# LayerNorm and MLP on one core: the first token tile in smaller pieces, b1 transposed first, and a first wave of five weight rows

## The chip, the core and the metric

The kernel runs on one core of a Trainium2 chip. A core has five engines that run their own instruction queues side by side: TensorE (PE, matrix multiplies into the accumulation memory PSUM, here eight banks), VectorE (DVE), ScalarE (ACT), GpSimd (POOL) and SyncE (SP, which here issues DMAs). Engines wait for each other and for DMAs by semaphores. The metric is the device time of one execution in microseconds (us); lower is better. The times of the kernel before are 399.81, 400.02 and 400.22 us, median 400.02.

## The reference

```python
y = _layernorm(x, axis=-1)                                    # x: 1 x 2048 x 1024, eps 1e-5
h = _gelu(jnp.einsum("bsd,df->bsf", y, w1) + b1)              # w1: 1024 x 3584, tanh form of gelu
return jnp.einsum("bsf,fd->bsd", h, w2) + b2                  # w2: 3584 x 1024
```

All inputs and the output are bfloat16. Counted in 128 x 128 blocks, the tokens make 16 tiles, the model dimension 8 contraction blocks (dt, 0 to 7) of the first product, and the hidden dimension 28 "rows" (r).

## The kernel before

Tokens are taken in four blocks of 512, each four tiles of 128. For a block, the first product computes for every hidden row r the 128 x 512 result sum over dt of w1[dt, r] against the transposed normalised tokens yT[dt], eight matmuls of 512 columns (line 354). ACT applies bias and GELU from PSUM into hT (L364). Then the second product (L397) runs, for each tile and each half of the 1024 outputs, 28 matmuls over the hidden rows; DVE adds b2 and stores to o_sb (L408), SP writes it out (L413). Five PSUM banks (ps_1, NB1) rotate for the first product, two (ps_2, NB2) for the second, and one (ps_t) takes transposes of the first block.

The program is first written as five lists of operations, one per engine, with named events; waits become semaphore waits when the lists are emitted. So the order in each list is the order in which the engine runs, and an operation that waits holds all behind it.

Block 0, the head, is special. Its four tiles arrive by their own DMAs. `SP_FIRST_LOADS` and `ACT_FIRST_LOADS` are the orders in which the SP and ACT queues issue the first loads; x0a and x0b are the column halves of tile 0, w0 to w3 are quarters of the first 512 columns of w1 (two column halves times two halves of dt). `ln_seq` puts the LayerNorm on DVE: for each tile two statistics (L253, one per column half) and an aggregate (L260); POOL raises to the power -0.5 (L257); then a subtract-and-multiply norm in place (L264). The norm of a tile stands on DVE behind the first statistics of the next tile:

```python
for h in range(2):
    seq.append(op_stats(i, h))
    if h == 0 and prev is not None:
        seq += ops_norm(prev)
seq.append(op_aggr(i))
```

Tile 0 is normalised in two halves of 512 columns, the others in one instruction of 1024. PE transposes a tile's eight 128 x 128 pieces into PSUM (L327, `pe_T`), and ACT copies them in two halves of 512 columns to yT (L333). PE also transposes b1 (L429), which ACT copies (L431), and runs warm-up matmuls on ones (L419): 26 free ones and then 8, 8 and 6 gated on steps of tile 0's LayerNorm.

The first product of block 0 starts with a "wave": four rows (`R_WAVE`), each with its own bank, are computed tile by tile with 128-column matmuls, so that work can start when one tile is there. For each tile, PE does the first four contraction blocks of the four rows, then the transposes of the next tile, then the other four blocks. The first matmul of each row of the wave waits for b1's copy as well. From row 4 on whole rows of 512 columns follow. Later blocks are normalised and transposed on DVE (L305) in gaps; a planner merges these operations with the evictions L408 by estimated due times (`est`, `pe_t`, `T_PE_START`). After the first loads, SP issues the rest of w1, x of block 1, w2, b2 and the other x.

## Time and profile before

| what | value |
|---|---|
| runs | 399.81, 400.02, 400.22 us |
| profiled execution, first to last instruction (span) | 398.3 us |
| median of the runs less that span | 1.7 us |
| PE busy | 394.9 us, 99% |
| PE on L354 and on L397 | 194.8 and 194.2 us |
| DVE, ACT, POOL busy | 137.3, 82.3, 9.7 us |
| DMA | 23.64 MB, most of it in the first 55 us |

The page gives no other time of the profiled execution than its span. The busy time of PE is modelled with pipelined ends, so it is read here by starts: how far two matmuls start apart. The stretch that matters is the first 16 us; all times in the text are counted from the first instruction of the profiled execution. "Landing" of a DMA is the time at which its semaphore is full.

### The profile page before, as it was taken

Reading aid. Unit: us, or ns where it says so; the run is one execution under the profiler, and the core shown is the slowest. Engines: PE = TensorE matmul, PEld = TensorE weight load, DVE = VectorE, ACT = ScalarE, POOL = GpSimd, SP = SyncE. Lnnn points to the kernel's source line nnn. Section 1 sums busy time; section 2 is a strip of 40 time slices with the busy share of each in tenths; the row PEclk is TensorE's granted clock in tenths of the full one; section 3 lists DMA queues with packets and bytes.
Section 4 is the critical chain, followed back from the end, with each engine's and each line's share of the span. In section 5 each row is a group of like instructions: output and inputs, shape, how many; then the busy total and the mean of one; then the engine's idle time right before and its main releaser. Section 6 shows DMA issues by size and latency. Waiting matters only on the chain.

```text
span 398.3 us, 4699 instructions
## 1 busy us (share of the span) xinstructions
PE 394.9 (99%) x2056; PEld 189.4 (48%) x2056; DVE 137.3 (34%) x292; ACT 82.3 (21%) x122; POOL 9.7 (2%) x25
## 2 busy tenths in 40 slices
PE   8999999999999999999999999999999999999998
PEld 7744444444444444444444444444444444444447
DVE  5207999899892004988100000001100000001011
ACT  3544430000044332000024334100003344400000
POOL 2002000200010000000000000000000000000000
DMA  8999930000000000000000000000000000000001
GB/s 255 369 387 386 385 146 15 26 13 29 26 1 2 0 0 2 26 15 26 27 15 0 0 2 0 1 27 26 13 28 13 2 0 0 2 13 26 15 26 28
DMA packets 17614, 23.64 MB, mean 59 GB/s; under 512 B 1466, under 2 KB 10042, under 8 KB 17594
## 3 DMA queue, kind: packets, MB, share of 16 engines
q1 hardware_dynamic: 17162, 22.95, 16.6%
q10 hardware_dynamic: 432, 0.39, 0.3%
q8 instruction: 16, 0.26, 0.3%
q14 instruction: 4, 0.03, 0.0%
HBM read 19.14 MB, written 4.19 MB: 59 GB/s over the span
## 4 chain that ended last, share of the span: by engine, by line
PE 99%; ACT 0%; issue 0%; DVE 0%; POOL 0%; POOLq 0%
PE ps L354 49%; PE ps L397 49%; PE ps L419 1%; PE ps_t L327 0%; ACT yT_sb L333 0%; DVE o_sb L408 0%; POOL ones L244 0%; ACT b_sb L431 0%; POOLq L525 0%
## 5 line engine op out<-in xcount | busy, mean ns | idle before, releaser
L354 PE MATMUL ps<-yT_sb,w_sb 128*128 128x512 bf16 (+1 forms) x992 | 194.8, 358 | 0.5 <-ACT b_sb L431 0.5
L397 PE MATMUL ps<-w_sb,hT_sb 128*128 128x512 bf16 (+1 forms) x980 | 194.2, 361 | 0.0
L354 PEld LDWEIGHTS ps<-yT_sb,w_sb 128*128 128x128 bf16 x992 | 91.7, 98 | 102.4 <-ACT b_sb L431 0.7
L397 PEld LDWEIGHTS ps<-w_sb,hT_sb 128*128 128x128 bf16 x980 | 91.3, 98 | 102.6
L364 ACT ACTIVATE hT_sb<-ps,b_sb 128x512 bf16<-128x512 f32 x112 | 76.7, 688 | 257.2 <-PE ps L354 257.2
L305 DVE STREAM_TRANSPOSE yT_sb<-x_sb 32x256 bf16<-32x256 bf16 x192 | 83.7, 436 | 35.0 <-PE ps L354 32.1
L408 DVE TENSOR_TENSOR o_sb<-ps,b_sb 128x512 bf16<-128x512 f32 (+1 forms) x35 | 22.6, 645 | 197.9 <-PE ps L397 197.8
L253 DVE BATCH_NORM_STATS2 st_sb<-x_sb 128x6 f32<-128x512 bf16 x32 | 21.1, 671 | 21.4 <-DMA x_sb<-in_x_dram 21.2
L257 POOL TENSOR_TENSOR rstd_sb<-mv_sb,nhalf 128x1 f32<-128x1 f32 x16 | 8.8, 551 | 111.5 <-DVE mv_sb L260 111.5
L264 DVE TENSOR_SCALAR x_sb<-x_sb,mv_sb,rstd_sb 128x1024 bf16<-128x1024 bf16 (+1 forms) x17 | 8.9, 528 | 3.7 <-POOL rstd_sb L257 2.7
L419 PE MATMUL ps<-ones 128*128 128x128 bf16 x51 | 5.4, 290 | 1.0 <-POOL ones L244 1.0
L419 PEld LDWEIGHTS ps<-ones 128*128 128x128 bf16 x51 | 4.6, 135 | 1.5 <-POOL ones L244 1.0
L333 ACT COPY yT_sb<-ps_t 128x512 bf16<-128x512 bf16 x7 | 3.8, 589 | 7.0 <-PE ps_t L327 7.0
L260 DVE BATCH_NORM_AGGREGATE mv_sb<-st_sb 128x2 f32<-128x15 f32 x16 | 3.6, 222 | 1.5
L327 PE MATMUL ps_t<-ident,x_sb 128*128 128x128 bf16 x28 | 2.2, 220 | 0.0
L422 ACT ACT_TABLE_LOAD x1 | 1.3, 1283 | 2.2 <-issue 2.2
L327 PEld LDWEIGHTS ps_t<-ident,x_sb 128*128 128x128 bf16 x28 | 1.7, 98 | 0.1
L333 ACT COPY yT_sb<-ps 128x512 bf16<-128x512 bf16 x1 | 0.6, 591 | 0.0
L327 PE MATMUL ps<-ident,x_sb 128*128 128x128 bf16 x4 | 0.4, 222 | 0.0
L245 POOL TENSOR_SCALAR_AFFINE_SELECT ident<-ones 128x128 bf16<-128x128 bf16 x1 | 0.3, 294 | 0.1
L327 PEld LDWEIGHTS ps<-ident,x_sb 128*128 128x128 bf16 x4 | 0.2, 98 | 0.1
L244 POOL MEMSET ones<- 128x128 bf16 x1 | 0.2, 205 | 0.3 <-POOLq L525 0.3
(10 smaller groups left out, 1.2 us busy)
## 6 DMA issues: line engine op xcount, KB each, us to landing
w_sb<-in_w_dram SPq DMA_DIRECT2D x4, 1792.0 KB, 18.5
w_sb<-in_w_dram SPq DMA_DIRECT2D x2, 2048.0 KB, 16.7
out_dram<-o_sb SPq DMA_DIRECT2D x31, 128.0 KB, 1.7
x_sb<-in_x_dram SPq DMA_DIRECT2D x3, 1024.0 KB, 14.2
w_sb<-in_w_dram SPq DMA_DIRECT2D x2, 1024.0 KB, 9.2
w_sb<-in_w_dram SPq DMA_DIRECT2D x4, 256.0 KB, 4.7
x_sb<-in_x_dram SPq DMA_DIRECT2D x2, 256.0 KB, 4.4
x_sb<-in_x_dram ACTq DMA_DIRECT2D x3, 128.0 KB, 3.7
```

The source lines that it names most:

```text
L253: return (lambda e, i=i, h=h: e.bn_stats(st_sb[:, i, 6 * h:6 * (h + 1)], x_sb[:, i, h * HC:(h + 1) * HC]), [x_ev[i][h]], f"st{i}_{h}", 0.65)
L257: pool.op(lambda e, i=i: e.tensor_tensor(out=rstd_sb[:, i:i + 1], in0=mv_sb[:, i, 1:2], in1=nhalf[:, i:i + 1], op=ALU.pow), waits=[f"mv{i} ...
L260: return (lambda e, i=i: e.bn_aggr(mv_sb[:, i, :], st_sb[:, i, :]), [f"st{i}_0", f"st{i}_1", "eps"], f"mv{i}", 0.33)
L264: return (lambda e, i=i, c0=c0, c1=c1: e.tensor_scalar(out=x_sb[:, i, c0:c1], in0=x_sb[:, i, c0:c1], scalar1=mv_sb[:, i, 0:1], scalar2=rst ...
L305: res.append((lambda e, src=src, dst=dst: e.transpose(out=dst, in_=src), waits, (f"tr{i}" if lastop else None), 0.47))
L327: pe.op(lambda e, i=i, j=j, bank=bank, o0=o0: e.transpose(out=bank[:, (j - o0) * P:(j - o0 + 1) * P], in_=x_sb[:, i, j * P:(j + 1) * P], i ...
L333: act.op(lambda e, dst=dst, src=src: e.copy(out=dst, in_=src), waits=[f"tp{i}_{h}" if i == 0 else f"tp{i}_{len(KGROUPS) - 1}"], sig=f"te{i ...
L354: pe.op(lambda e, b=b, r=r, dt=dt, n0=n0, n1=n1, bank=bank: e.matmul(ps_1[:, bank, n0:n1], lhsT=w1_sb[:, dt, r * P:(r + 1) * P], rhs=yT_sb ...
L364: act.op(lambda e, r=r, n0=n0, n1=n1, bank=bank: e.activation(out=hT_sb[:, r, n0:n1], in_=ps_1[:, bank, n0:n1], func=ACT.Gelu_apprx_tanh, ...
L397: pe.op(lambda e, st=st, ft=ft, c0=c0, c1=c1, bank=bank: e.matmul(ps_2[:, bank, 0:c1 - c0], lhsT=hT_sb[:, ft, st * P:(st + 1) * P], rhs=w2 ...
L408: crit.append((est[sig], (lambda e, ob=ob, c0=c0, c1=c1, bank=bank: e.tensor_tensor(out=o_sb[:, ob, c0:c1], in0=ps_2[:, bank, 0:c1 - c0], ...
L419: pe.op(lambda e: e.matmul(ps_2[:, NB2 - 1, 0:P], lhsT=ones[:, :], rhs=ones[:, :], start=True, stop=True), waits=["ones"] + ([gate] if gat ...
```

## The change

The changes are in the head of the program, in block 0 and in the order of the first loads.

- b1 is transposed and copied first, ahead of tile 0's transposes in PE's and ACT's lists; its load moves from third on SP's queue to fourth on ACT's. Only the wave's row 4, whose bank b1's transpose uses, and the GELUs wait for it.
- Tile 0 is normalised in pieces of 256 and 768 columns (`NORM_0`), and transposed and copied in groups of 2, 3 and 3 contraction blocks (`GROUPS_0`), each with a bank of its own (ps_t and the two banks of ps_2). Four instead of three warm-up matmuls (into ps_1) stand between the first group and the others.
- Tiles 1 to 3 are normalised in two halves (`NORM_1`) and transposed in two groups of four (`GROUPS_1`), each waiting for its own half and copied as soon as it is transposed.
- The wave has five rows instead of four. Within a tile the order is by contraction block, and by row inside it; the groups of the next tile's transposes come ahead of blocks 6 and 7. The last tile goes row by row.
- The w1 columns of the wave (640) come in four pieces by contraction block (two blocks each, rows of 1280 bytes), w0 to w3; the rest in pieces of 384, 1024, 1024 and 512 columns. x2 is loaded in halves, x2a behind w2 and x2b behind w3.
- After the five banks of ps_1, units six and seven of the first product use the two banks of ps_2 once; the first output groups wait for their GELUs.

```diff
 P = 128
 TB = 512
 TPB = TB // P
-R_WAVE = 4
-K_GROUPS = 2
+R_WAVE = 5
 NB1 = 5
 NB2 = 2
 NOB = 2
 TAIL_PIECES = 4
 WARM_A = ((26, None), (8, "st0_0"), (8, "mv0"), (6, "rstd0"))
-N_WARM_B = 3
-W1_CHUNK_COLS = (256, 256, 512, 512, 1024, 1024)
-W1_KSPLIT_CHUNKS = 2
+N_WARM_B = 4
+NORM_0 = (0, 2, 8)
+GROUPS_0 = (0, 2, 5, 8)
+NORM_1 = (0, 4, 8)
+GROUPS_1 = (0, 4, 8)
+W1_WAVE_KSPLIT = 4
+W1_REST_COLS = (384, 1024, 1024, 512)
 N_W2_CHUNKS = 4
-SP_FIRST_LOADS = ("x0a", "x2", "b1", "w0", "w1", "w2", "w3", "x3", "w4")
-ACT_FIRST_LOADS = ("x0b", "x1a", "x1b")
-
-T_PE_START = 8.5
+SP_FIRST_LOADS = ("x0a", "w0", "w1", "w2", "x2a", "w3", "x2b", "x3", "w4")
+ACT_FIRST_LOADS = ("x0b", "x1a", "x1b", "b1")
+
+T_PE_START = 6.9
 T_DVE_START = 13.0
 DMA_T0 = 2.1
 DMA_BYTES_PER_US = 0.34e6
...
     HC = D // 2
     assert ST % TB == 0 and D % P == 0 and F % P == 0 and D % NCH == 0
     assert HC <= 512 and DT * P * 2 <= 2048 and FT >= 4 and FT <= P
-    R = max(1, min(R_WAVE, FT - 2, NB1 - 1))
-    nkg = max(1, min(K_GROUPS, DT))
-    KGROUPS = [(h * DT // nkg, (h + 1) * DT // nkg) for h in range(nkg)]
-    assert NB1 + NB2 + 1 <= 8
+    R = max(1, min(R_WAVE, FT - 2, NB1))
+    assert NB1 + NB2 + 1 <= 8 and NB2 == 2
+    assert all(c[-1] == DT for c in (NORM_0, GROUPS_0, NORM_1, GROUPS_1))
 
     w1_chunks = []
-    c0 = 0
-    for n, wdt in enumerate(W1_CHUNK_COLS):
-        if c0 + wdt <= F:
-            if n < W1_KSPLIT_CHUNKS:
-                for j0, j1 in KGROUPS:
-                    w1_chunks.append((j0, j1, c0, c0 + wdt))
-            else:
-                w1_chunks.append((0, DT, c0, c0 + wdt))
-            c0 += wdt
-    while c0 < F:
-        c1 = min(F, c0 + 512)
-        w1_chunks.append((0, DT, c0, c1))
+    for h in range(W1_WAVE_KSPLIT):
+        w1_chunks.append((h * DT // W1_WAVE_KSPLIT, (h + 1) * DT // W1_WAVE_KSPLIT, 0, R * P))
+    c0 = R * P
+    for wdt in W1_REST_COLS + (512,) * (F // 512 + 1):
+        c1 = min(F, c0 + wdt)
+        if c1 > c0:
+            w1_chunks.append((0, DT, c0, c1))
         c0 = c1
 
     def w1_chunk_of(r, dt):
...
         y_ev = {}
 
         def ops_norm(i):
-            if i == 0:
-                y_ev[i] = [f"y{i}_{h}" for h in range(2)]
-                return [op_norm(i, h * HC, (h + 1) * HC, f"y{i}_{h}") for h in range(2)]
-            y_ev[i] = [f"y{i}"] * 2
-            return [op_norm(i, 0, D, f"y{i}")]
+            cuts = NORM_0 if i == 0 else NORM_1 if i < TPB else (0, DT)
+            y_ev[i] = []
+            res = []
+            for k, (j0, j1) in enumerate(zip(cuts[:-1], cuts[1:])):
+                res.append(op_norm(i, j0 * P, j1 * P, f"y{i}_{k}"))
+                y_ev[i] += [f"y{i}_{k}"] * (j1 - j0)
+            return res
 
         def ln_seq(tiles):
             seq = []
...
 
         def ops_T(i):
             blk, t = divmod(i, TPB)
-            waits = list(y_ev[i])
+            waits = [y_ev[i][-1]]
             if blk - 2 in mm1_done:
                 waits.append(mm1_done[blk - 2])
             res = []
...
             dve.op(o[0], waits=o[1], sig=o[2])
 
         pe_t = [T_PE_START]
-        last_te = [None]
-
-        def pe_T(i):
+        bank_read = {}
+        t_banks = [("t", ps_t[:, 0, :]), ("2_0", ps_2b[:, 0, :]), ("2_1", ps_2b[:, 1, :])]
+
+        def pe_T(i, groups, k):
             blk, t = divmod(i, TPB)
-            evs = []
-            for h, (j0, j1) in enumerate(KGROUPS):
-                own = i == 0 and h == 1
-                bank = ps_2b[:, 0, :] if own else ps_t[:, 0, :]
-                o0 = j0 if own else 0
-                waits = [y_ev[i][h], "ident"]
-                if h == 0 and last_te[0] is not None:
-                    waits.append(last_te[0])
-                for j in range(j0, j1):
-                    pe.op(lambda e, i=i, j=j, bank=bank, o0=o0: e.transpose(
-                        out=bank[:, (j - o0) * P:(j - o0 + 1) * P], in_=x_sb[:, i, j * P:(j + 1) * P],
-                        identity=ident[:, :]),
-                        waits=waits if j == j0 else (), sig=(f"tp{i}_{h}" if j == j1 - 1 else None))
-                src = bank[:, (j0 - o0) * P:(j1 - o0) * P].rearrange("p (j s) -> p j s", j=j1 - j0)
-                dst = yT_sb[:, blk % 2, j0:j1, t * P:(t + 1) * P]
-                act.op(lambda e, dst=dst, src=src: e.copy(out=dst, in_=src),
-                       waits=[f"tp{i}_{h}" if i == 0 else f"tp{i}_{len(KGROUPS) - 1}"], sig=f"te{i}_{h}")
-                evs += [f"te{i}_{h}"] * (j1 - j0)
-            yT_ev[i] = evs
-            last_te[0] = evs[-1]
+            j0, j1 = groups[k], groups[k + 1]
+            bname, bap = t_banks[k]
+            evs = yT_ev.setdefault(i, [None] * DT)
+            for j in range(j0, j1):
+                waits = []
+                if j == j0:
+                    waits = ["ident"] + ([bank_read[bname]] if bname in bank_read else [])
+                if j == j0 or y_ev[i][j] != y_ev[i][j - 1]:
+                    waits.append(y_ev[i][j])
+                pe.op(lambda e, i=i, j=j, o=(j - j0) * P, bap=bap: e.transpose(
+                    out=bap[:, o:o + P], in_=x_sb[:, i, j * P:(j + 1) * P], identity=ident[:, :]),
+                    waits=waits, sig=(f"tp{i}_{k}" if j == j1 - 1 else None))
+                evs[j] = f"te{i}_{k}"
+            src = bap[:, 0:(j1 - j0) * P].rearrange("p (j s) -> p j s", j=j1 - j0)
+            dst = yT_sb[:, blk % 2, j0:j1, t * P:(t + 1) * P]
+            act.op(lambda e, dst=dst, src=src: e.copy(out=dst, in_=src), waits=[f"tp{i}_{k}"], sig=f"te{i}_{k}")
+            bank_read[bname] = f"te{i}_{k}"
+            pe_t[0] += (j1 - j0) * 0.056
 
         unit_n = [0]
-        unit_gelu = []
+        bank_gelu = {}
+        first_ring = [("1", k) for k in range(NB1)] + [("2", 1), ("2", 0)]
 
         def new_unit():
             u = unit_n[0]
             unit_n[0] += 1
-            return u % NB1, ([unit_gelu[u - NB1]] if u >= NB1 else ["b1c"])
+            bank = first_ring[u] if u < len(first_ring) else ("1", (u - len(first_ring)) % NB1)
+            waits = [bank_gelu[bank]] if bank in bank_gelu else []
+            if bank == ("1", NB1 - 1) and not waits:
+                waits.append("b1c")
+            if bank[0] == "2" and not waits:
+                waits.append(bank_read[f"2_{bank[1]}"])
+            return bank, waits
+
+        def unit_bank(bank):
+            return (ps_1 if bank[0] == "1" else ps_2)[:, bank[1], :]
 
         def pe_cell(b, r, t0, t1, bank, waits, sig, dts=None):
             n0, n1 = t0 * P, t1 * P
...
                 w = (waits if k == 0 else []) + [f"w1c{w1_chunk_of(r, dt)}"]
                 w += [yT_ev[b * TPB + t][dt] for t in range(t0, t1)]
                 pe.op(lambda e, b=b, r=r, dt=dt, n0=n0, n1=n1, bank=bank: e.matmul(
-                    ps_1[:, bank, n0:n1], lhsT=w1_sb[:, dt, r * P:(r + 1) * P], rhs=yT_sb[:, b % 2, dt, n0:n1],
+                    unit_bank(bank)[:, n0:n1], lhsT=w1_sb[:, dt, r * P:(r + 1) * P], rhs=yT_sb[:, b % 2, dt, n0:n1],
                     start=(dt == 0), stop=(dt == DT - 1)),
                     waits=w, sig=(sig if dt == DT - 1 else None))
             pe_t[0] += len(dts) * _mm_us(n1 - n0)
...
         def act_gelu(r, t0, t1, bank, wait_ev, sig):
             n0, n1 = t0 * P, t1 * P
             act.op(lambda e, r=r, n0=n0, n1=n1, bank=bank: e.activation(
-                out=hT_sb[:, r, n0:n1], in_=ps_1[:, bank, n0:n1], func=ACT.Gelu_apprx_tanh,
+                out=hT_sb[:, r, n0:n1], in_=unit_bank(bank)[:, n0:n1], func=ACT.Gelu_apprx_tanh,
                 bias=b1_sb[:, r:r + 1], scale=1.0),
                 waits=[wait_ev, "b1c"], sig=sig)
-            unit_gelu.append(sig)
+            bank_gelu[bank] = sig
 
         hT_row = {}
 
...
             waits = [f"w2c{ci}" for ci in range(nw2c)]
             if g >= NB2:
                 waits.append(grp_oe[g - NB2])
+            else:
+                waits.append(bank_gelu[("2", bank)])
             for ft in range(FT):
                 pe.op(lambda e, st=st, ft=ft, c0=c0, c1=c1, bank=bank: e.matmul(
                     ps_2[:, bank, 0:c1 - c0], lhsT=hT_sb[:, ft, st * P:(st + 1) * P], rhs=w2_sb[:, ft, c0:c1],
...
 
         def warm(n, gate=None):
             for _ in range(n):
-                pe.op(lambda e: e.matmul(ps_2[:, NB2 - 1, 0:P], lhsT=ones[:, :], rhs=ones[:, :],
+                pe.op(lambda e: e.matmul(ps_1[:, 0, 0:P], lhsT=ones[:, :], rhs=ones[:, :],
                                          start=True, stop=True), waits=["ones"] + ([gate] if gate else []))
 
         act.op(lambda e: e.preload_act_table(ACT.Gelu_apprx_tanh))
...
         for o in ln_seq(list(range(TPB))):
             dve_put(o)
 
-        pe_T(0)
         pe.op(lambda e: e.transpose(out=ps_1b[:, NB1 - 1, 0:FT], in_=b1r_sb[:, :], identity=ident[0:FT, 0:FT]),
               waits=["ident", "b1"], sig="b1t")
         act.op(lambda e: e.copy(out=b1_sb[:, :], in_=ps_1b[:, NB1 - 1, 0:FT]), waits=["b1t"], sig="b1c")
+        pe_T(0, GROUPS_0, 0)
         warm(N_WARM_B)
+        for k in range(1, len(GROUPS_0) - 1):
+            pe_T(0, GROUPS_0, k)
         wave = [new_unit() for _ in range(R)]
         for t in range(TPB):
             lastt = (t == TPB - 1)
-            for h, (j0, j1) in enumerate(KGROUPS):
-                for r in range(R):
-                    sig = f"m1_0_{r}" if lastt else f"m1_0_{r}_w{t}"
-                    pe_cell(0, r, t, t + 1, wave[r][0], wave[r][1] if (t == 0 and h == 0) else [], sig,
-                            dts=range(j0, j1))
-                    if lastt and j1 == DT:
-                        act_gelu(r, 0, TPB, wave[r][0], sig, f"g_0_{r}")
-                        hT_row[(0, r)] = f"g_0_{r}"
-                if t + 1 < TPB and h == 0:
-                    pe_T(t + 1)
-                    pe_t[0] += DT * 0.056
+            order = [(r, dt) for r in range(R) for dt in range(DT)] if lastt else \
+                [(r, dt) for dt in range(DT) for r in range(R)]
+            for r, dt in order:
+                if not lastt and r == 0 and dt >= DT - 2:
+                    pe_T(t + 1, GROUPS_1, dt - (DT - 2))
+                sig = f"m1_0_{r}" if lastt else f"m1_0_{r}_w{t}"
+                pe_cell(0, r, t, t + 1, wave[r][0], wave[r][1] if (t == 0 and dt == 0) else [], sig, dts=[dt])
+                if lastt and dt == DT - 1:
+                    act_gelu(r, 0, TPB, wave[r][0], sig, f"g_0_{r}")
+                    hT_row[(0, r)] = f"g_0_{r}"
 
         def mm1_rows(b, r0):
             for r in range(r0, FT):
```

## The prediction

> **What bounds the kernel now.** I read the waits first, then the chain in order of time, then the head on the timelines of TensorE (PE), VectorE (DVE) and ScalarE (ACT), and the DMA issues last. All waits of PE behind a finished warm-up:
>
> ```profile
> PE ps L354 <- ACT b_sb L431: 0.5, 1, 0.5
> ```
>
> PE waits once, before its first real matmul, and never again up to its last one at 396.45. So the span is: start of the first real matmul, plus PE's work, plus 1.8 us of eviction and store. A change in the head is worth what it moves that start, less new PE stalls, less new PE work. The chain in order of time shows the start:
>
> ```profile
> 6.09 0.36 PE ps_t L327 x4
> 6.47 1.07 ACT yT_sb L333 x2
> 7.54 0.10 ACT b_sb L431
> 7.69 1.07 PE ps L354 x16
> 8.75 0.45 PE ps_t L327 x8
> ```
>
> Two copies of tile 0 (L333), then the copy of b1 (L431), lead to 7.69. The timelines give the durations used below (start, duration; first PE, then ACT, then DVE):
>
> ```profile
> 5.81 0.28 PE L419 MATMUL ps<-ones 128*128 128x128 bf16 x2
> 6.36 0.40 PE L327 MATMUL ps<-ident,x_sb 128*128 128x128 bf16 x4
> 6.69 0.18 PE L429 MATMUL ps<-ident,b1r_sb 28*128 28x28 bf16 x1
> 6.81 0.34 PE L419 MATMUL ps<-ones 128*128 128x128 bf16 x3
> ...
> 6.95 0.59 ACT L333 COPY yT_sb<-ps 128x512 bf16<-128x512 bf16 x1
> 7.43 0.20 ACT L431 CAST b_sb<-ps 128x28 f32<-128x28 bf16 x1
> ...
> 4.97 0.69 DVE L253 BATCH_NORM_STATS2 st_sb<-x_sb 128x6 f32<-128x512 bf16 x1
> 5.59 0.72 DVE L264 TENSOR_SCALAR x_sb<-x_sb,mv_sb,rstd_sb 128x512 bf16<-128x512 bf16 x2
> 7.15 0.64 DVE L253 BATCH_NORM_STATS2 st_sb<-x_sb 128x6 f32<-128x512 bf16 x1
> 7.91 0.55 DVE L264 TENSOR_SCALAR x_sb<-x_sb,mv_sb,rstd_sb 128x1024 bf16<-128x1024 bf16 x1
> ```
>
> Warm 128-column matmuls and transposes start 0.056 apart (8 transposes take 0.45, 32 matmuls 1.79); one ends 0.22 after its start. ACT starts 0.04 after PE ends (6.43, 6.47), PE 0.06 after ACT ends (7.63, 7.69).
>
> **The start.** DVE's order is kept: tile 1's first statistics at 4.97, then tile 0's norm at 5.59. A 512-column norm lasts 0.40, a 1024-column one 0.55, so 256 columns last about 0.33 and are ready at 5.92; the pair still takes DVE 0.63, as before. PE's last gated warm-up starts at 5.87. Next in its queue is now b1's transpose: before, it started 0.15 behind the transpose ahead of it (6.54, 6.69) and 0.12 before its successor, so 6.02 and then tile 0's first two transposes at 6.14 and 6.20, the last ending at 6.42. ACT does b1's copy at 6.24 to 6.44, then the 256-column copy from 6.46. Copies: 0.59 for 512 columns and 0.20 for 28, so 0.38 for 256 and 0.49 for 384. It ends at 6.84, the first matmul starts at 6.90: 0.79 gained. Its waits no longer name b1's copy, which row 4 alone needs, at 7.12; it is there at 6.44.
>
> The four warm-ups and the six other transposes follow (6.26 to 6.78); the 384-column copies end at 7.35 and 7.73, for contraction blocks 2 (due 7.46) and 5 (due 8.30). Hidden, by 0.05 us at the least after the 0.06 handover.
>
> **Work added.** Row 4 of block 0 becomes 32 cells of 128 columns, 32 x 0.056 = 1.79, for eight of 512, 1.73 (starts of GELUs are 1.73 apart): +0.06. The transposes are as many as before.
>
> **The handover between tiles, new.** A tile's 40 cells are ordered by contraction block over five rows; the next tile's transposes come in two fours ahead of blocks 6 and 7. From the first four's start, the copy needs 0.17 + 0.22 + 0.04 + 0.59 + 0.06 = 1.07 until the next tile's block 0 can start, while PE has 18 instructions, 1.01. That is a wait of 0.06, three times: +0.18. Before, 16 matmuls followed all eight transposes, and PE had no wait there.
>
> **Tile 1, where part of the gain goes.** PE reaches tile 1's transposes 30 cells after its start: 6.90 + 1.68 = 8.58. They need tile 1's norm, and on DVE that norm stands behind tile 2's first statistics. Before, x2 was SP's second load and those statistics ran at 7.15 without a wait; now x2a stands behind w0, w1 and w2, and a DVE that waits for it holds the norm of tile 1. The loads, issue to landing (x0b is issued at 0.78, x1a at 1.21, x1b at 1.70, w3 at 3.73, x3 at 4.28, w4 at 5.39):
>
> ```profile
> x_sb<-in_x_dram ACTq DMA_DIRECT2D x1, 128.0 KB, 3.7
> w_sb<-in_w_dram SPq DMA_DIRECT2D x1, 256.0 KB, 5.1
> x_sb<-in_x_dram SPq DMA_DIRECT2D x1, 256.0 KB, 5.3
> w_sb<-in_w_dram SPq DMA_DIRECT2D x1, 1024.0 KB, 7.2
> ```
>
> By x1b (5.40) 0.793 MB had landed, by w3 (8.83) 1.842, by x3 (9.58) 2.104, by w4 (12.59) 3.153: 0.306 MB/us for the 512-byte rows of w0 to w3, 0.35 for the 1 KB rows of w4. The new pieces have rows of 1280 bytes, nearest to the latter: I take 0.35. Up to and with w2 there are 1.515 MB, x2a 1.646, w3 1.974, x2b 2.105, x3 2.367; landings 7.46, 7.84, 8.77, 9.15, 9.90. From x2a: 0.04 to start, 0.61 of statistics, 0.40 of a 512-column norm, 0.06 to PE: transposes at 8.95, a stall of 0.37. Bounds: at 0.387 MB/us, the best of the page's 40 slices, 7.60 and a stall of 0.12; at 0.306, 8.19 and 0.72. Without the wait for x2a the norm would start at 7.91 as before and the transposes at 8.37 at the earliest: no stall. The stall also covers w3, due at 8.95 + 0.22 = 9.17. Pieces w1 and w2 land at 6.53 and 7.46 for blocks 2 and 4, due 7.46 and 8.02.
>
> **Tiles 2 and 3.** Norms in two pieces take DVE 0.63 for 0.46. Tile 2: second statistics 9.19, POOL's power done 10.83, its first half ready near 11.3, due at 8.95 + 1.07 + 1.68 = 11.70. Tile 3 about 13.7, due near 14.4. Hidden, by 0.4 and 0.7.
>
> **Costed at nothing.** SP still issues nine first loads; ACT issues one more (0.45) and its table load moves to about 3.9, work there begins at 6.24. The piece of 384 columns lands by 12.6, due past 17; the next (2.1 MB) near 18.5, due 22.9. Units six and seven take banks of the second group, long read by then; the first output groups wait on GELUs that end some 35 us before. Earlier due times reorder DVE's fill work by about 1 us; DVE is busy 105 of the last 341 us. POOL's queue keeps its order.
>
> **The sum** against the profiled span of 398.3: -0.79 + 0.37 + 0.18 + 0.06 = -0.18. The median of the runs is 1.72 above that span; I add this unchanged: 399.84, so 399.8. With the bounds of x2a: -0.43 to +0.17, 399.6 to 400.2.
>
> **Rivals.** *All loads in time.* x2a lands by 7.47 and w3 by 8.76: no stall at tile 1, sum -0.79 + 0.18 + 0.06 = -0.55, 399.5. For it: SP's queue now lacks b1's 256-byte rows and 512-byte rows. Against: it needs 0.41 MB/us from x1b on, more than any slice has; only a quicker start before 5.40 could bring part of it.
>
> *b1 late, the slower side.* b1 stood third on SP and landed before 6.69; it now is fourth on ACT's queue, behind x1b, and PE's queue stops at its transpose, with tile 0 behind it. From its landing the first matmul is 0.06 + 0.12 + 0.06 + 0.22 + 0.04 + 0.38 + 0.06 = 0.94 away. A landing up to 5.96 is free; up to 6.3 it hides in the stall of tile 1; from 6.50 the kernel is slower than before, from 7.3 by over 0.2%. If both queues share evenly, b1 lands shortly after x1b, 5.5 to 5.9. If they take turns by whole transfers (w0, x1a, w1, x1b, w2, b1), it lands with w2, 7.46: start 8.40, stall gone, +0.71 + 0.18 + 0.06 = +0.95, 401.0. Traffic of 3.0 to 3.5 speaks for turns (x2 on q1 goes ahead of x1a on q10):
>
> ```profile
> q1 hardware_dynamic: 64, 0.13, 101.8%
> q10 hardware_dynamic: 10, 0.01, 5.7%
> ```
>
> Against whole turns: x1a, ACT's second, landed at 4.91, only 0.2 behind x2 (1.23 + 3.5), where its 0.131 MB alone, moved after all of x2, would take 0.4.
>
> [...]
>
> *Five banks in turn cost PE.* If a matmul into another bank than the one before took 0.066 for 0.056 (the step behind a wait), 160 cells cost 1.6 more: 401.4. Against: at the changes of row in the present wave the step stays 0.056.
>
> **How the numbers follow.** Stall at tile 1 as costed 0.60; all in time 0.15; b1 late 0.16, of which 0.11 beyond 0.2%; five banks 0.03; faster by over 0.2% needs a start before 6.65 with no stall, for which I can name nothing: 0.06. About 0.2%, 0.8 us, is what a measurement tells from no change. Faster 0.06, same 0.79, slower 0.15 (b1, banks, a small rest). Range 399.4 to 400.8: from the case in time to most of b1's, leaving out its worst, the banks and the unnamed gain.
>
> **What would show it.** First L354 matmul at 6.9; L429 ahead of the L327s near 6.0, with no wait on b1; DVE waiting for x_sb before tile 2's statistics near 7.9; PE waiting for DVE before the transposes near 8.9; three waits on L333 of 0.06. Wrong if b1's transpose waits for DMA past 6.3, or if PE waits for w_sb.

## The result and the profile after

The changed kernel is slower, by little: median 400.30 us of 18 executions, against 399.95 of 18 of the kernel before on the same chips; ratio 1.002, 95% interval 1.0011 to 1.0030. The ratio, here and below, lies close to that of the means, to which a few late executions add; the medians here differ by 0.35 us, 0.09%. I had forecast 399.8 against 400.02, a gain of 0.2. Fourteen of the 18 lie between 399.96 and 400.60; four lie at 401.8 to 402.7, and the profiled one, 402.66 with a span of 401.4, is one of these four; the kernel before has none so far above its median.

The waits of the changed kernel's profiled execution, of TensorE's matmuls (PE) and of its weight loads (PEld): who waits for whom, us in total, times, longest.

```profile
PE ps L438 <- DMA b1r_sb<-in_b_dram: 2.1, 1, 2.1
...
PEld ps L362 <- ACT yT_sb L333: 0.3, 1, 0.3
```

The same execution's chain of work that ended last, in order of time (start, us, what):

```profile
2.21 5.88 DMA b1r_sb<-in_b_dram
8.09 0.05 issue
8.13 0.20 PE ps L438
8.33 0.33 PE ps_t L327 x2
8.66 0.43 PE ps L429 x4
9.09 0.64 PE ps L327 x6
9.72 2.41 PE ps L362 x30
```

The chain no longer runs through tile 0's LayerNorm. It runs through the load of b1, issued at 2.21 and landed at 8.09, and PE stands 2.05 us at b1's transpose (L438), with tile 0's transposes behind it. The semaphore events tell why so late: 14 of the 15 updates that the DMA makes are there by 6.74, the last at 8.09; w1's first 15 parts by 6.55, its last at 8.29. One part of each is 1.3 to 1.7 us late; that one DMA engine fell behind is my guess, for the trace names no engine beside a part.

A second thing is seen in the steps: four warm-ups from 8.66 on take 0.43, 0.107 each, where they took 0.056 before the wait. The windows of the same execution show it as the granted clock; the first line is that view's heading:

```profile
core 0: us, PE busy (x) PEld busy (x) DVE busy (x) ACT busy (x) POOL busy (x), PEclk, DMA share, GB/s
9.00:12.00 3.00, 3.00 (x38) 3.00 (x37) 2.33 (x6) 0.93 (x3) 0.63 (x2) 0.64 1.09 350
```

So this profile alone can't tell what the change does in the usual execution. The first experiment is therefore the changed kernel again.

### The profile page after: what moved, and what is told of

It is laid out like the page before. It is cut to its first block, busy times and chain, and to the rows that moved or that the text cites. A ratio compares the mean times of both kernels' runs of the same rounds, so it can differ in the third digit from the quotient of the medians.

```text
span 401.4 us, 4753 instructions
## 1 busy us (share of the span) xinstructions
PE 396.2 (99%) x2081; PEld 191.4 (48%) x2081; DVE 138.3 (34%) x295; ACT 82.5 (21%) x123; POOL 9.7 (2%) x25
## 4 chain that ended last, share of the span: by engine, by line
PE 97%; DMA 1%; ACTq 0%; ACT 0%; DVE 0%; issue 0%
PE ps L362 48%; PE ps L407 48%; DMA b1r_sb<-in_b_dram 1%; ACTq L179 0%; ACT yT_sb L333 0%; PE ps L327 0%; PE ps_t L327 0%; PE ps L429 0%; DVE o_sb L418 0%; PE ps L438 0%
## 5 line engine op out<-in xcount | busy, mean ns | idle before, releaser
L362 PEld LDWEIGHTS ps<-yT_sb,w_sb 128*128 128x128 bf16 x1016 | 93.8, 99 | 101.2 <-ACT yT_sb L333 0.3
L261 DVE TENSOR_SCALAR x_sb<-x_sb,mv_sb,rstd_sb 128x1024 bf16<-128x1024 bf16 (+3 forms) x20 | 9.5, 490 | 3.8 <-POOL rstd_sb L254 2.7
L333 ACT COPY yT_sb<-ps_t 128x512 bf16<-128x512 bf16 (+1 forms) x4 | 2.1, 534 | 5.6 <-PE ps_t L327 5.4
L333 ACT COPY yT_sb<-ps 128x512 bf16<-128x512 bf16 (+1 forms) x5 | 2.6, 544 | 0.4 <-PE ps L327 0.4
L438 PE MATMUL ps<-ident,b1r_sb 28*128 28x28 bf16 x1 | 0.2, 199 | 2.1 <-DMA b1r_sb<-in_b_dram 2.1
L327 PE MATMUL ps<-ident,x_sb 128*128 128x128 bf16 x18 | 2.0, 251 | 0.0
L327 PEld LDWEIGHTS ps<-ident,x_sb 128*128 128x128 bf16 x18 | 1.5, 116 | 0.0
L438 PEld LDWEIGHTS ps<-ident,b1r_sb 28*128 28x128 bf16 x1 | 0.1, 100 | 2.2 <-DMA b1r_sb<-in_b_dram 2.2
```

The lines of the kernel that those rows point to most:

```text
L261: return (lambda e, i=i, c0=c0, c1=c1: e.tensor_scalar(out=x_sb[:, i, c0:c1], in0=x_sb[:, i, c0:c1], scalar1=mv_sb[:, i, 0:1], scalar2=rst ...
L327: pe.op(lambda e, i=i, j=j, o=(j - j0) * P, bap=bap: e.transpose(out=bap[:, o:o + P], in_=x_sb[:, i, j * P:(j + 1) * P], identity=ident[:, ...
L333: act.op(lambda e, dst=dst, src=src: e.copy(out=dst, in_=src), waits=[f"tp{i}_{k}"], sig=f"te{i}_{k}")
L362: pe.op(lambda e, b=b, r=r, dt=dt, n0=n0, n1=n1, bank=bank: e.matmul(unit_bank(bank)[:, n0:n1], lhsT=w1_sb[:, dt, r * P:(r + 1) * P], rhs= ...
```

## The experiments

Four theories were set against each other. A: PE's start hangs on b1's landing. B: the five-row wave and its transposes cost the time. T: b1 lands late because the SP and ACT queues take turns by whole transfers. D: the wave's last tile has a wait that I had not costed. Each run was timed beside the kernel before on its chip. "Start" is the first real matmul of the profiled execution; "wave" is from there to the place of row 5 (the last matmul's end less 378.51, which is the same in every five-row profile; a wave of four rows is followed by row 4 in 1.73 and ends 380.24 before the end). All times in us.

| kernel | start | wave | median | before beside it | ratio, 95% interval |
|---|---|---|---|---|---|
| before (first profile) | 7.69 | 8.52 + 1.73 | | | |
| changed, first profile | 9.52 | 11.55 | 400.30 | 399.95 | 1.0020, 1.0011 to 1.0030 |
| changed again (e0) | 7.70 | 10.83 | 400.26 | 399.77 | 1.0015, 1.0007 to 1.0024 |
| b1 second on SP (e1) | 7.54 | 11.91 | 400.91 | 399.77 | 1.0023, 1.0015 to 1.0032 |
| b1 behind tile 0 (e2) | 7.21 | 11.26 | 399.95 | 399.77 | 1.0010, 1.0000 to 1.0020 |
| before, b1 first (e3) | 7.61 | 9.16 + 1.73 | 399.75 | 399.77 | 0.9996, 0.9988 to 1.0005 |
| last tile in halves (e4) | 8.01 | 10.48 | 400.13 | 399.85 | 1.0005, 0.9996 to 1.0014 |
| e2, e4 and early norm 1 (e5) | 7.63 | 10.63 | 399.60 | 399.85 | 0.9992, 0.9984 to 1.0001 |
| b1 behind w3 (e6) | 10.48 | 11.63 | 404.01 | 399.85 | 1.0104, 1.0091 to 1.0118 |
| e6 with warm-ups (e7) | 10.44 | 10.77 | 402.95 | 399.85 | 1.0085, 1.0071 to 1.0099 |
| e5, fewer warm-ups (e8) | 7.32 | 10.70 | 399.80 | 399.93 | 0.9997, 0.9988 to 1.0006 |
| e5, four rows (e9) | 7.39 | 10.11 + 1.73 | 400.65 | 399.93 | 1.0018, 1.0009 to 1.0026 |
| b1 second on ACT (e10) | 10.13 | 12.81 | 403.18 | 399.93 | 1.0066, 1.0043 to 1.0089 |
| eight w1 pieces (e11) | 6.97 | 12.04 | 399.83 | 399.81 | 1.0001, 0.9992 to 1.0010 |
| e11, e4, early norm 1 (e12) | 7.37 | 10.53 | 399.77 | 399.76 | 0.9998, 0.9989 to 1.0007 |
| e12, b1 behind tile 0 (e13) | 7.53 | 10.64 | 399.98 | 399.76 | 1.0001, 0.9992 to 1.0009 |

**The changed kernel again (e0).** No edit.

> The changed kernel once more, for a second profile. Theory A (b1's landing sets the start: PE stands at b1's transpose, tile 0 behind it): without the late DMA engine of the first profile b1's transpose runs near 6.8, the first real matmul near 7.7, about where it was before, and the kernel is 0.2 to 0.3 us slower than before (the handover waits 0.18 and row 4 0.06). Rival B (the five-row wave and its transposes cost the time): the first real matmul is at 6.9 to 7.1 and PE waits more than 0.8 us in all at the transposes and the cells of tiles 1 to 3.

In its chain, b1's load and transpose:

```profile
2.20 4.50 DMA b1r_sb<-in_b_dram
6.70 0.04 issue
6.75 0.18 PE ps L438
```

In its timeline (start, us, engine, line, operation, out<-in), PE's last warm-ups and PE from there through the wave; an idle time would stand in brackets at the end of a line:

```profile
4.22 2.42 PE L429 MATMUL ps<-ones 128*128 128x128 bf16 x21
6.75 0.18 PE L438 MATMUL ps<-ident,b1r_sb 28*128 28x28 bf16 x1
...
7.70 1.83 PE L362 MATMUL ps<-yT_sb,w_sb 128*128 128x128 bf16 x30
9.43 0.40 PE L327 MATMUL ps_t<-ident,x_sb 128*128 128x128 bf16 x4
...
12.19 0.39 PE L327 MATMUL ps_t<-ident,x_sb 128*128 128x128 bf16 x4
...
14.94 0.39 PE L327 MATMUL ps_t<-ident,x_sb 128*128 128x128 bf16 x4
```

DVE in the same timeline, with the wait ahead of tile 1's norm:

```profile
8.36 0.69 DVE L250 BATCH_NORM_STATS2 st_sb<-x_sb 128x6 f32<-128x512 bf16 x1 [0.44 <-DMA x_sb<-in_x_dram]
8.97 0.72 DVE L261 TENSOR_SCALAR x_sb<-x_sb,mv_sb,rstd_sb 128x512 bf16<-128x512 bf16 x2
```

And its weight loads in the wave's last tile:

```profile
16.50 0.28 PEld L362 LDWEIGHTS ps<-yT_sb,w_sb 128*128 128x128 bf16 x5 [0.28 <-ACT yT_sb L333]
```

Without the late part b1 lands at 6.70 and the start is 7.70, within 0.01 of where the profile of the kernel before had it. Theory A holds, though b1 explains only part of this one start: PE's last gated warm-up starts at 6.41 here, at 5.87 in the profile of before, and b1 then holds PE for 0.19 more; in e4, with the same loads, it holds it for 0.60. Theory B falls: from the start on the waits are 0.05 at tile 1 (9.43, due 9.38), three handovers of 0.06, and one of 0.28 that I had not seen: in the last tile, which goes row by row, PE comes to block 4 of row 0 after four cells, at 16.23, and the second copy of that tile ends at 16.45. DVE did wait 0.44 for x2a with tile 1's norm behind it, as forecast, but the late start covers all of it but 0.05.

**b1 out of the start's way (e1, e2).** e1 loads b1 early, e2 transposes it behind tile 0's cells.

```diff
-SP_FIRST_LOADS = ("x0a", "w0", "w1", "w2", "x2a", "w3", "x2b", "x3", "w4")
-ACT_FIRST_LOADS = ("x0b", "x1a", "x1b", "b1")
+SP_FIRST_LOADS = ("x0a", "b1", "w0", "w1", "w2", "x2a", "w3", "x2b", "x3", "w4")
+ACT_FIRST_LOADS = ("x0b", "x1a", "x1b")
```

> The changed kernel with b1 loaded second on SP's queue instead of fourth on ACT's; nothing else differs. Theory A: b1 lands near 5, the first real matmul starts at 6.9 to 7.1, tile 1's transposes then wait for tile 1's norm, held behind x2a, until about 9.0; about 0.4 us faster than the changed kernel and 0.1 to 0.3 faster than the kernel before (399.7), and no execution 2 us above the others. Rival B: no faster than the changed kernel by more than 0.1 us.

```diff
-        pe.op(lambda e: e.transpose(out=ps_1b[:, NB1 - 1, 0:FT], in_=b1r_sb[:, :], identity=ident[0:FT, 0:FT]),
-              waits=["ident", "b1"], sig="b1t")
-        act.op(lambda e: e.copy(out=b1_sb[:, :], in_=ps_1b[:, NB1 - 1, 0:FT]), waits=["b1t"], sig="b1c")
...
+            if t == 0:
+                pe.op(lambda e: e.transpose(out=ps_2b[:, 1, 0:FT], in_=b1r_sb[:, :], identity=ident[0:FT, 0:FT]),
+                      waits=["ident", "b1", bank_read["2_1"]], sig="b1t")
+                act.op(lambda e: e.copy(out=b1_sb[:, :], in_=ps_2b[:, 1, 0:FT]), waits=["b1t"], sig="b1c")
+                bank_read["2_1"] = "b1c"
```

> The changed kernel with b1's transpose and copy moved behind tile 0's cells, into the second bank of ps_2, its load left fourth on ACT's queue. Theory A: no wait for b1 anywhere; first real matmul at 6.9 to 7.0, tile 1's transposes wait until about 9.0, so 0.1 to 0.3 us faster than before (399.7), like the early load. Rival B: as slow as the changed kernel.

e2 starts at 7.21 and is 0.31 faster than the changed kernel, as A has it; the rest of the start's gain stops at tile 1, where PE now waits for the norm behind x2a, in e2's timeline:

```profile
7.21 1.83 PE L360 MATMUL ps<-yT_sb,w_sb 128*128 128x128 bf16 x30
9.21 0.40 PE L327 MATMUL ps_t<-ident,x_sb 128*128 128x128 bf16 x4 [0.16 <-DVE x_sb L261]
```

I had expected it to be faster than the kernel before, and it isn't: the 0.28 of the last tile and 0.12 for b1's transpose were missing in that expectation. Two of its 12 executions took 401.5 and 401.7 at a mean clock of 1.000, so b1 at the start is not the only source of late executions.

e1 refuted me: it is 0.65 slower than the changed kernel. b1 came early and b1's transpose no longer waits, but its windows show a hole in the transfers, 125 GB/s (the last number) from 3.25 to 4.75:

```profile
3.25:4.75 1.50, 1.16 (x12) 0.90 (x11) 1.17 (x2) 0.25 (x1) 0.00 (x0) 1.00 0.59 125
```

The same window of the changed kernel (e0):

```profile
3.25:4.75 1.50, 1.36 (x14) 1.10 (x12) 1.29 (x2) 0.97 (x1) 0.00 (x0) 1.00 1.01 340
```

Every later load on SP's queue lands about 1 us later (x1a and x1b, on ACT's, 1.1 and 0.8 earlier), and DVE waits for x2a with tile 1's norm behind it, in e1's timeline:

```profile
9.29 0.69 DVE L250 BATCH_NORM_STATS2 st_sb<-x_sb 128x6 f32<-128x512 bf16 x1 [1.75 <-DMA x_sb<-in_x_dram]
```

Until PE waits too, in the same timeline:

```profile
10.35 0.40 PE L327 MATMUL ps_t<-ident,x_sb 128*128 128x128 bf16 x4 [0.68 <-DVE x_sb L261]
```

**The kernel before with b1 first (e3).** The two lines of b1 are moved ahead of `pe_T(0)`; its load stays third on SP.

> The kernel before with b1 transposed and copied ahead of tile 0; its load and all else as before. The first real matmul can start near 7.2 instead of 7.7. Theory A, with the LayerNorms as the next bound: tile 1's norm is ready at 8.45 and tile 2's at 10.78, so their transposes can't start before 8.51 and 10.84, where they start already (8.59, 10.84): 0 to 0.1 us faster. Rival C (the start alone counts): 0.5 us faster, 399.5.

There is no gain, but this doesn't decide between the two: in its profile the start is 7.61, only 0.08 earlier, with the last gated warm-up at 6.17 (5.87 in the profile of before). Nor is my reason what it shows: PE waits 0.38 for tile 0's copy and then 0.47 for a piece of w1, and the norms are in time. That piece had one part at 8.63 and the others by 8.06, when it was due (8.05), so one profile doesn't make w1's loads the next bound. In e3's timeline:

```profile
7.61 0.61 PE L354 MATMUL ps<-yT_sb,w_sb 128*128 128x128 bf16 x8 [0.38 <-ACT yT_sb L333]
8.68 0.62 PE L354 MATMUL ps<-yT_sb,w_sb 128*128 128x128 bf16 x8 [0.47 <-DMA w_sb<-in_w_dram]
```

**The last tile (e4).**

```diff
-            order = [(r, dt) for r in range(R) for dt in range(DT)] if lastt else \
+            order = [(r, dt) for d0 in (0, DT // 2) for r in range(R) for dt in range(d0, d0 + DT // 2)] if lastt else \
```

> The changed kernel, with the wave's last tile in two halves of contraction blocks (blocks 0 to 3 of all five rows, then 4 to 7 of each row) instead of row by row. In the second profile of the changed kernel PE starts the last tile at 16.0 and needs the second copy of that tile four cells later, at 16.23, but it ends at 16.45. Theory D (this wait of 0.28 us is a loss of its own): 0.25 to 0.3 us faster than the changed kernel, about 400.0. Rival: no difference over 0.1 us, because the GELUs or the copies bound the end of the wave.

PE's weight loads in the last tile, with no wait at 16.5 (e4's timeline):

```profile
15.85 1.12 PEld L362 LDWEIGHTS ps<-yT_sb,w_sb 128*128 128x128 bf16 x18
```

Theory D holds in the trace. The wave is 10.48, which is its 184 steps of 0.056, 10.29, and the three handovers, 0.19, and nothing else; the changed kernel's is 10.83. The distance of the medians to the kernel before falls from 0.49 to 0.28, though the two intervals overlap. In this profile b1's transpose ran at 7.05, so the start alone was 0.3 later than in e0.

**The losses together (e5), and what five rows are worth (e9).** e5 takes e2 and e4, and puts tile 1's norm ahead of tile 2's first statistics; e9 is e5 with `R_WAVE = 4`.

```diff
                 seq.append(op_aggr(i))
                 prev = i
+                if i == 1:
+                    seq += ops_norm(1)
+                    prev = None
```

> The changed kernel with three edits: b1's transpose behind tile 0's cells (as in the run with that edit alone, 399.95), the last tile in two halves, and on DVE tile 1's norm ahead of tile 2's first statistics, so that x2a no longer holds it. If the losses add (theory A with D and the hold by x2a): start near 7.2, tile 1's transposes at 8.9 without a wait, tile 2's wait some 0.1 for its norm; 0.28 + 0.3 - 0.1 better than 399.95: 399.4 to 399.5, 0.3 us faster than before. Rival: the next LayerNorm takes the gain back, 399.8 to 400.0.

> The same kernel (399.6) with a wave of four rows instead of five. If five rows are what gives the LayerNorms and copies their time: a tile's cells take 1.79 us plus 0.45 of transposes, the handover waits 1.07 - 0.90 = 0.17 three times, and tile 2's transposes, due 2.4 behind tile 1's, wait for a norm that follows 2.9 behind: 0.3 to 0.9 us slower, 399.9 to 400.5. Rival (the fifth row only adds 0.06 of work): equal or 0.06 faster.

e5 is 0.74 below the changed kernel by the distance to the kernel before (+0.49 for the changed kernel, -0.25 for e5, with an interval that just includes no difference). No PE wait for a norm is left. e9 loses about 1 us against it: with four rows PE waits for tile 1's and for tile 2's norm, and longer at two handovers (0.17 for 0.06). In e9's waits:

```profile
PE ps_t L330 <- DVE x_sb L261: 0.6, 2, 0.3
```

Five rows are no cost of the change; they are what makes room for the LayerNorms.

**A longer wait, with and without work for PE (e6, e7).** b1 is loaded on SP behind w3; e7 adds `warm(54)` ahead of its transpose.

> The changed kernel with b1 loaded on SP behind w3: the suspected wait made longer on purpose. Theory A: b1 lands near 9.3, PE idles some 3.3 us, the first real matmul is 0.94 behind the landing, near 10.3, and the kernel loses 2.6 us against the changed one by the start alone. If an idle of 2 us or more also halves the step of PE (0.107 for 0.056, as in the first profile of the changed kernel, where PE had idled 2.05 us), a further 0.8 to 2 us is lost, for 35 to 60 instructions at 0.05 each: 403.5 to 405 in all. Rival: the wait is absorbed at tile 1, under 401.

> The same late load of b1, with 54 more warm-up matmuls (3 us) ahead of b1's transpose, so that PE is busy while b1 is on its way. The start is near 10.3 as in the run without them; if idleness of PE costs the step, all steps from b1's transpose on are 0.056 here and the kernel is 0.8 to 2 us faster than the run without the warm-ups, near 402.7. Rival (the halved step has nothing to do with idleness): both are equal.

The starts are 10.48 and 10.44 (b1 lands at 9.05 and 9.35); yet e6 is 1.06 slower, by medians of four and five executions. PE's wait in e6's timeline:

```profile
9.10 0.20 PE L438 MATMUL ps<-ident,b1r_sb 28*128 28x28 bf16 x1 [2.67 <-DMA b1r_sb<-in_b_dram]
```

The window from 9 to 12 of e6, with the columns as above:

```profile
9.00:12.00 3.00, 2.90 (x28) 2.87 (x29) 2.79 (x7) 1.42 (x4) 0.55 (x1) 0.50 1.09 348
```

And of e7:

```profile
9.00:12.00 3.00, 3.00 (x51) 2.73 (x49) 2.70 (x8) 1.42 (x4) 0.55 (x1) 1.00 1.11 356
```

After 2.67 us of idleness PE got half its clock and did 28 instructions where it did 51 when kept busy. This is what the four slow executions of the changed kernel have in common by their mean clock (0.996 against 1.000). That in all four it was a late b1 is seen in the profiled one only.

**Why b1 lands late (e11, e10).** e11 keeps the order of bytes but cuts the wave's w1 into eight pieces.

```diff
-W1_WAVE_KSPLIT = 4
+W1_WAVE_KSPLIT = 8
...
-SP_FIRST_LOADS = ("x0a", "w0", "w1", "w2", "x2a", "w3", "x2b", "x3", "w4")
+SP_FIRST_LOADS = ("x0a", "w0", "w1", "w2", "w3", "w4", "w5", "x2a", "w6", "w7", "x2b", "x3", "w8")
```

> The changed kernel with the wave's w1 in eight pieces (one contraction block each, 164 KB) instead of four (328 KB); the order of bytes on SP and all else as in the changed kernel, b1 fourth on ACT's queue. Theory T (the two queues take turns by whole transfers, so b1, ACT's fourth, lands behind SP's third or fourth): with pieces half as long b1 lands 0.4 to 0.7 us earlier, its transpose runs at 6.1 to 6.4 instead of 6.75, the first real matmul at 7.1 to 7.3. The end moves less, 0 to 0.3 us, because tile 1's norm is held by x2a (as before) to about 9.2. Rival (the queues share by bytes): b1's transpose stays at 6.6 to 6.9.

PE in e11's timeline:

```profile
6.02 0.18 PE L438 MATMUL ps<-ident,b1r_sb 28*128 28x28 bf16 x1
6.13 0.29 PE L327 MATMUL ps_t<-ident,x_sb 128*128 128x128 bf16 x2
...
6.97 1.83 PE L362 MATMUL ps<-yT_sb,w_sb 128*128 128x128 bf16 x30
...
12.66 0.40 PE L327 MATMUL ps_t<-ident,x_sb 128*128 128x128 bf16 x4 [0.91 <-DVE x_sb L261]
```

Theory T holds in its direction: with the same order of bytes, in pieces half as long, b1 lands at 5.97 instead of 6.70, hardly holds PE any more, and the start is 6.97, 0.07 from what I had predicted for the change. It is more than one profile: with 328 KB pieces b1 landed at 6.69 to 7.10 (e0, e2, e4, e5, e8; 8.09 in the first profile), with 164 KB pieces at 5.96 to 6.37 (e11 to e13); e9, with pieces of 262 KB, has 7.32 and doesn't fit between. The kernel gains about 0.45 on the changed one by the distance to the kernel before, and is equal to that. The 0.91 at tile 2 is x3, one part of which came 1.2 late in this execution (400.64, over the median by 0.8).

In e10 b1 is second on ACT's queue: `("x0b", "b1", "x1a", "x1b")`.

> The changed kernel with b1 second on ACT's queue (x0b, b1, x1a, x1b) instead of fourth. With b1 second on SP's queue, b1 came early, but from 3.25 to 4.75 us only 125 GB/s moved where the changed kernel moves 340, and all later loads came 0.9 to 1 us late. Theory H (a load of b1's form ahead of others makes what is queued behind it start late): x1a and x1b land 0.5 to 1 us later than in the changed kernel, tile 0's norm, which stands behind x1a's statistics, starts near 6.4 instead of 5.9, the first real matmul is at 7.5 or later, and the kernel is not faster than the changed one (400.2 to 400.8). Rival (b1's 7 KB cost next to nothing): first real matmul at 7.0 to 7.2, 0.3 faster than the changed kernel, 399.9.

b1's transpose runs at 6.10 without a wait, but x1a, issued at 1.94 right behind b1, lands 5.9 later, and x1b 6.5 after its issue. The line of DMA issues in e10 (queue, size, us from issue to landing):

```profile
x_sb<-in_x_dram ACTq DMA_DIRECT2D x1, 128.0 KB, 5.9
```

And what PE then waits for, in e10's timeline:

```profile
8.88 0.40 PE L327 MATMUL ps_t<-ident,x_sb 128*128 128x128 bf16 x2 [2.59 <-DVE x_sb L261]
```

Theory H (a load of b1 put ahead holds up what stands behind it) has the direction. Its size, 400.2 to 400.8, is near that of four of the 11 executions (400.3 to 401.3); the other seven took 403.1 to 404.7 at a mean clock of 0.996 or less, and the profiled one, 404.54, is one of them. In it tile 0's norm, behind x1a's statistics, comes 2.6 later than in e0, and the clock halves again (PEclk 0.50 from 9 to 12). H's own mechanism isn't shown by this, for theory T gives most of it: x1a is now third on ACT's queue, and the third load there, x1b, landed at 6.88 in e0, so 1.6 of the 2.6 is what that place cost there. The rest lies in four of x1a's 16 parts, which came at 7.08 to 7.86 where the others were there by 6.27.

What is left for H is e1's hole, and a small load ahead of large ones doesn't always make one: in e6, with b1 on the same queue behind w3, x2b, x3 and w4 behind it landed at 9.25, 9.92 and 12.32 (in e0 at 9.56, 10.28 and 12.65). Why the transfers fall to 125 GB/s in e1 is not settled.

**On top of eight pieces (e12, e13), and fewer warm-ups (e8).** e12 adds e5's early norm and e4's order to e11; e13 also moves b1's transpose behind tile 0; e8 is e5 with gated warm-ups of 8, 6 and 2 instead of 8, 8 and 6.

> Eight w1 pieces, with tile 1's norm ahead of tile 2's first statistics and the last tile of the wave in two halves; b1's transpose is first, as in the changed kernel. If the three terms are the whole account: first real matmul near 7.0, tile 1's transposes near 8.65 without a wait, tile 2's with a wait of 0.1 at most, no wait in the last tile: 0.4 to 0.6 us faster than the kernel before. If a bound behind them takes it back: a wait of 0.3 or more for tile 2's norm in the typical execution and 0.2 faster at most.

> The same with b1's transpose behind tile 0's cells instead of first. If b1's place costs nothing once it lands before tile 0's norm is ready: equal within 0.1 us, its one transpose costing 0.12 in either place. If its landing still reaches past the norm in some executions: faster by 0.1 to 0.3 and with fewer slow executions.

> The kernel with late b1, tile 1's norm early and the last tile in halves (399.6), with 8, 6 and 2 gated warm-ups instead of 8, 8 and 6. In the profile of that kernel PE stood in warm-ups at a step of 0.107 until 6.6, while tile 0's first norm piece was ready at 6.15. Theory E (the queue of warm-ups is the next bound of the start): first transposes at 6.2, first real matmul near 7.2, 0.2 to 0.4 us faster than that kernel, 399.3. Rival: with fewer warm-ups the step of PE stays at 0.107 longer, and the first cells lose as much or more: 399.6 to 400.5.

All three are equal to the kernel before within their intervals; of the 0.4 to 0.6 that I expected of e12, its interval reaches 0.4 at its very end. In e12's profile the wave's waits are gone (10.53 = 10.48 and 0.05 at tile 2), but the start is 7.37, not 6.97, and b1 sets it once more. In e12's chain:

```profile
2.18 4.19 DMA b1r_sb<-in_b_dram
6.37 0.05 issue
6.42 0.18 PE ps L441
```

b1 lands at 6.37 here, 0.4 later than in e11, while tile 0's first piece is normalised at 6.05 and the last gated warm-up starts at 6.14. e13 doesn't wait for b1, and its start is 7.53, behind the warm-ups; in its timeline:

```profile
4.38 2.48 PE L430 MATMUL ps<-ones 128*128 128x128 bf16 x22 [0.39 <-DVE st_sb L250]
```

They wait for x0a's statistics, which began at 3.63 here and at 3.23 in the profile of the kernel before, and they run at a step of 0.107 up to the last, at 6.65, when tile 0's first piece is long normalised (6.26). In the profile of before the step fell to 0.056 at 5.48. The warm-ups bound the start in e1, e2, e5, e9 and e13 alike, where b1 doesn't hold it and none of them is left out: the last one starts at 6.33 to 6.65, and the piece is ready at 6.07 to 6.26. e11's early start had the last one at 5.84, as early as the profile of before (5.87). e8 took six of them away; there the piece, ready at 6.42, bounds it. Its start of 7.32 lies within those of e2, e5, e9 and e13 (7.21 to 7.63), so one profile doesn't show that it gained, and the median did not; its times spread from 399.3 to 400.9. No version tried is clearly faster than the kernel before; e5 comes nearest, at 0.9992.

## Why the prediction was wrong

By its own terms, in the second profile of the changed kernel against the profile of before:

| term | predicted | measured |
|---|---|---|
| start | -0.79 | +0.01 |
| tile 1's norm behind x2a | +0.37 | +0.05 |
| three handovers | +0.18 | +0.19 |
| row 4 | +0.06 | +0.06 |
| last tile, row by row | not costed | +0.28 |
| sum | -0.18 | +0.59 (397.04 less 396.45, PE's last end) |

The medians beside each other give +0.49 on that chip. The row of the start holds a difference between executions too: from PE's last gated warm-up (5.87 in the profile of before, 6.41 here) to the first real matmul it is 1.82 before, 1.29 here and 1.03 in the prediction.

The step that failed is the term of the start, -0.79: it stands on a b1 that lands by 5.96, and b1 landed at 6.70 here and at 6.69 to 7.10 in the five profiles with these loads and no late part. My own sign of being wrong, b1's transpose waiting past 6.3, came true. I had this as the rival "b1 late" and gave it 0.16. Its mechanism was written down and is what happened; its price, 0.94 from landing to start, nearly holds (1.00 in e0, e4, e11 and e12). What was wrong is where I took b1 to land: "shortly after x1b, 5.5 to 5.9" for even sharing. x1b itself, 5.40 before, lands at 6.88 in the second profile, where SP's queue has w0 and w1 (320 KB each, landed at 5.3 and 7.10) in the places of x2 and b1. I had the row that spoke for turns (x2's 64 packets ahead of x1a's 10 from 3.0 to 3.5), and discarded it on one difference of landings, 0.2 us, which is smaller than the spread of one transfer's own sixteen parts (0.62 for x1a in the profile of before, 4.33 to 4.95). Pieces half as long brought the landing down to between 5.96 and 6.37 (e11 to e13); in e11 it is 0.73 earlier than in e0, where theory T had 0.4 to 0.7. Whole turns as I had listed them are not what happened, for in e0 b1 came with x1b and w1 (6.88 and 7.10) and not with w2 (7.94); no run here shows how large a turn is.

The same term has a second fault: it took the last gated warm-up, 5.87, from one profile. With b1 out of the way the start is 7.21 to 7.63 (e2, e5, e9, e13) and not 6.90, because that warm-up starts at 6.33 to 6.65 there. e11 came near 6.90 with that warm-up at 5.84. How far the kernel before shares this in its usual executions isn't shown by its one profile.

The absorption worked as predicted: the late start covered tile 1's stall. The LayerNorm chain itself was rightly followed: from x2a's landing I had 1.11 to the transposes, measured 1.09 (8.34 to 9.43); x2a landed at 8.34 for the predicted 7.84. The terms of the handover add up to 1.08, not 1.07; the wait was 0.06 each time, as forecast.

The last tile's wait is a step left out: I described its order and did not compare the second copy with the fourth cell. All numbers for it stood in the prediction (a copy of 0.59 behind another, 0.056 per cell).

The rivals of banks in turn (+1.6) and of all loads in time did not occur; a matmul into another bank keeps its step of 0.056 (e0's first 30 cells over five banks, 1.83 with 0.22 for the last to end). The range held the 14 usual executions but not the tail: I had considered idle time of PE only for what it delays, not for what it does to the clock. And the sum was set against one profile of the kernel before whose span, 398.3, is one of the shortest of its executions (398.1 to 399.5 beside the experiments); the usual one is 398.5, and what lies around the span is about 1.3, not the 1.72 I added.

## What to carry to other kernels

Before a small load is made the first thing that an in-order engine waits for, find its place in its queue and see what the other queue issues ahead of it: b1, fourth on ACT's queue, landed at 6.69 to 7.10 beside 328 KB pieces on SP's, and at 5.96 to 6.37 beside 164 KB pieces. Moving it to the front of a queue can delay what follows by far more than its bytes (about 1 us in e1, for 7 KB), and every load that it passes moves back a place. A gain at the start is only worth what the next waits leave of it: list for every tile what is due when, and look at the tile where the order of the loop changes. In the head of a kernel, compare several executions before a sum of tenths is trusted.

## What the runs showed of the hardware

- PE's clock halved after 2.05, 2.59 and 2.67 us of idleness (step 0.107, PEclk 0.50 to 0.64 in the window from 9 to 12; first profile, e10, e6) and not after 0.6 (e4) or 0.9 (e11), where the step behind is 0.056; the price was 1.06 us here (e6 against e7).
- PE's first matmuls run at the same step of 0.107, although PEclk reads 1.00 there (14 matmuls from 4.75 to 6.00 in e5). In the profiles the step fell to 0.056 at times between 4.3 (e3) and 7.1 us (e5), which moves the end of the warm-ups and with it the start (last gated warm-up and start 5.84 and 6.97 in e11, 6.65 and 7.53 in e13).
- The same load landed at another time when the other queue held other loads: x1b, third on ACT's queue, at 5.40 in the kernel before and at 6.88 in e0, and b1 behind it at 6.69 to 7.10 with 328 KB pieces on SP's queue and at 5.96 to 6.37 with 164 KB pieces.
- A 7 KB load in 28 rows of 256 bytes, second on SP's queue, was followed by 1.5 us at 125 GB/s, where the same window has 340 without it (e1, e0); behind w3 on that queue it delayed nothing (e6: x2b behind it landed at 9.25, in e0 at 9.56).
- One of the parts of a transfer was now and then 1.2 to 1.9 us later than the others (the first profile's loads from w1 on, 1.3 to 1.9; x3 in e11, 1.2); in the first profile, where the first work waits for such a transfer, the execution was 2.4 us over the median.
